# The opening of a gated-attention kernel: first four outputs from transposed strips of their own score panels, with the weights and v of batch 1 loaded later and z of batch 1 transposed later

## The chip, the cores and the metric

The kernel runs on one core of one Trainium2 chip. The metric is device time in microseconds (us) of one execution, inputs and outputs in HBM. Each comparison runs both kernels several times on the same chip. A run is called slow here when it is over 1.5% above the fastest run of the same kernel in its comparison. The granted clock is the share of TensorE's full clock that the profile shows as allowed.

Names: PE is the TensorE matmul engine, DVE is VectorE, ACT is ScalarE, POOL is GpSimd, SP is SyncE. SP issues the DMA transposes, POOL issues almost all loads and stores. In profile lines, PEld is PE's loading of weights, SPq is SP's DMA queue, and L12 is line 12 of that kernel, so one source line has different numbers in different kernels.

## The reference, cut to what matters

Batch 8, sequence S = 3136, model width 256, score width 64, rank 32.

```python
scores = (z @ z^T) / S                    # symmetric, 3136 x 3136, per batch
attn   = maximum(scores, 0) ** 2
x      = u * (attn @ v)                   # gated attention
h      = x^T @ U @ V                      # rank-32 mixing over the sequence
y      = x + h^T
out    = y + maximum(y @ w_ch1, 0) @ w_ch2
```

## The kernel before

The sequence is cut into 25 tiles of 128 rows (the last has 64). The scores are symmetric, so a panel `A[j]` holds only 13 of the 25 blocks of its row: its own and the next 12, wrapping round. For output tile o, 13 blocks come straight from stored panels, and the other 12 come from a DMA transpose of the panel of o itself, called a strip. Work goes by output tile in the order 12, 13, ..., 24, 0, ..., 11; the position in that order is called `i`. "Tile 24" below means output o = 24, which stands at position 12; a load or transpose "at tile 12" means at position i = 12. In the code NT = 25, NF = 24, HALF = FIRST = 12, P = 128 and B = 8. The mixer and the two large products of batch b run inside the attention of batch b + 1.

```python
def score(b, parts):                    # scores into PSUM, then relu on ACT, square on DVE
    ps = pair_psum()
    ...                                 # cut: one or two matmuls from zT
    for dst, src in todo:
        nc.scalar.activation(out=dst, in_=src, func=AF.Relu, scale=sc)
    for dst, _ in todo:
        nc.vector.tensor_tensor(out=dst, in0=dst, in1=dst, op=ALU.mult)

def turn(b, o):                         # a strip: 12 blocks transposed by DMA, on SP's queue
    strip = strip_pool.tile([P, HALF, P], BF16, name="strip")
    transpose(out=strip, in_=A[o][:, P:])
    strips[b, o] = strip

def block(b, o, j):
    k = (o - j) % NT
    return A[j][:, k * P : (k + 1) * P] if k <= HALF else strips[b, o][:, NT - 1 - k, :]
```

The opening of batch 0 (`start_up`) makes outputs 12 to 15 from freshly scored columns, without strips, and puts a marker on SP's queue that holds the first strips until batch 1's first v parts have landed. The large loads are issued near its top.

```python
def start_up():
    parts = ((8, 16), (0, 8), (16, NF))
    first_z(parts[:2])
    ...                                 # cut: identity, v of batch 0, z turned on PE
    if B > 1:
        load_z(1, WHOLE)
    run(fetches)                        # w1, U, V, two halves of w2: 1.4 MB in the SBUF types
    if B > 1:
        for part in V_PARTS[:3]:
            load_v(1, part)             # 3 x 192 KB
    ...
    pairs = [(8, 9), (10, 11), (12, 13), (14, 15), (6, 7), (3, 4), (5,), (1, 2)]
    pairs += [(0, 16), (17, 18), (19, 20), (21, 22), (23, 24)]
    ...
    for i, pair in enumerate(pairs):
        if i == 5 and B > 1:            # the marker
            nc.sync.dma_start(out=mark, in_=v_both[1][:1, V_PARTS[2][1] - 1, :8])
        ...
        make(pair)
        if i > 5 and i % 2:
            nxt.pop(0)()
        if i > 1:
            use(pairs[i - 2], outs)
    ...                                 # cut: outputs 16 to 19, from panels and strips
        if B > 1 and i in (1, 2):       # z of batch 1, doubled and transposed here, issued at 40 to 44 us
            part = ((0, FIRST), (FIRST, NF))[i - 1]
            double_z(1, (part,))
            turn_z(1, (part,))
```

After the opening each batch runs its tiles with one strip issued per tile, four tiles ahead. From tile 13 the panels of the next batch are scored among the attention matmuls, which needs the transposed z (`zT`) of that batch:

```python
for i in range(begin, NT):              # begin = 8 in batch 0
    o = turns(i)
    fill = [s for key in own.get(i, ()) for s in score_steps(b, *key)]
    if more:
        fill += [s for key in next_at[i] for s in score_steps(b + 1, *key)]   # from i = 13
        if b and i == 7:
            turn_z(b + 1, ((FIRST, NF),))
        if b and i == 10:
            turn_z(b + 1, ((0, FIRST),))
        ...
    _spread(attend_steps(b, o), fill)
    if i + AHEAD < NT:
        turn(b, turns(i + AHEAD))
```

Of the kernel before, what the change touches and what calls it, by code (L numbers as in the profile page):

```python
# [42 lines left out]
def kernel(  # L43
# [156 lines left out]
    def first_z(parts):  # L200

        z_bf = z_tiles[0] = stage.tile([P, NT, 2, dqk], BF16, name="z_bf")
        wide = zT_rest[:, :4, :].rearrange("p t c -> p (t c)")
        nc.vector.memset(wide, 0.0)
        ps = pair_psum()
        for _ in range(7):
            mm(out=ps[:, 0, :], lhsT=zT_rest[:, 0, :], rhs=wide, start=True, stop=True)
        landed = []
        for t0, t1 in parts:
            z_f = u_pool.tile([P, 2, D], FP32, name="u_sb").rearrange("p a c -> p (a c)")  # L210
            z_f = z_f.rearrange("p (t c) -> p t c", c=dqk)
            nc.sync.dma_start(out=z_f, in_=rows(z[0])[:, t0:t1, :])
            landed.append(z_f)
        for (t0, t1), z_f in zip(parts, landed):
            nc.vector.tensor_copy(out=z_bf[:, t0:t1, 0, :], in_=z_f)
            nc.scalar.copy(out=z_bf[:, t0:t1, 1, :], in_=z_f)

    def turn_on_pe(parts, banks):

        z_bf = z_tiles[0]  # L220
        for (t0, t1), ps in zip(parts, banks):
            for t in range(t0, t1):
                mm(
                    out=ps[:, (t - t0) * P : (t - t0 + 1) * P],
                    lhsT=z_bf[:, t, :, :].rearrange("p h c -> p (h c)"),
                    rhs=eye,
                    start=True,
                    stop=True,
                )
            copy = nc.vector.tensor_copy if t0 % 8 or t1 == NF else nc.scalar.copy  # L230
            copy(
                out=zT_first[:, t0:t1, :].rearrange("p t c -> p (t c)"),
                in_=ps[:, : (t1 - t0) * P],
            )
# [424 lines left out]

    def start_up():  # L660
        parts = ((8, 16), (0, 8), (16, NF))
        first_z(parts[:2])
# [10 lines left out]
        load_v(0, (8, 12))  # L673
        load_v(0, (12, 18))
        load_z(0, parts[2:])
        for part in [(3, 8), (0, 3), (18, NF), (NF, NT)]:
            load_v(0, part)
        turn_on_pe([(8, 12), (12, 16)], sets[0])
        turn_on_pe([(0, 4), (4, 8)], sets[1])
        nc.gpsimd.memset(U_bf[:, NF, :], 0.0)  # L680
        outs = [FIRST + i for i in range(NG)]
        c0 = FIRST * P
        for o in outs[::2]:
            open_pair(0, o)
            load_u(0, o)
        if B > 1:
            load_z(1, WHOLE)
        run(fetches)
        if B > 1:
            for part in V_PARTS[:3]:  # L690
                load_v(1, part)
        nxt = [s for j in range(LEAD, LEAD + NG) for s in turned(0, j)]
        rooms = [A[j % NT][:, : 2 * NG * P] for j in range(LEAD + NG, LEAD + 3 * NG)]
        rooms = [r.rearrange("p (a w) -> p a w", a=2) for r in rooms]
        pairs = [(8, 9), (10, 11), (12, 13), (14, 15), (6, 7), (3, 4), (5,), (1, 2)]
        pairs += [(0, 16), (17, 18), (19, 20), (21, 22), (23, 24)]
        where = {}
        mark = small.tile([P, D], BF16, name="mark", tag="t1_sb")[:1, :8]

        def make(pair):  # L700
            if all(LEAD - 1 - HALF <= j < FIRST for j in pair):
                todo = []
                for j in pair:
                    at = (FIRST - j) * P
                    where[j] = A[j][:, at : at + NG * P]
                    todo.append((j, c0, NG * P, where[j]))
                score(0, todo)
            else:
                room = rooms.pop(0)
                for i, j in enumerate(pair):  # L710
                    where[j] = room[:, i, :]
                score(0, [(j, c0, NG * P, room) for j in pair])

        def use(pair, some):
            for j in pair:
                for o in some:
                    at = (o - FIRST) * P
                    stop = [o % 2 == 1 and j == NF - h for h in range(2)]
                    beside(o, j, where[j][:, at : at + P], stop)

        for i, pair in enumerate(pairs):
            if i == 5 and B > 1:

                nc.sync.dma_start(out=mark, in_=v_both[1][:1, V_PARTS[2][1] - 1, :8])
            if i == 3:
                double_z(0, parts[2:])
            if i == 5:
                turn_on_pe([(16, NF)], [pair_psum().rearrange("p a w -> p (a w)")])
                turn_on_pe([(NF, NT)], [pair_psum()[:, 0, :]])
                extend_z(0)  # L730
            make(pair)
            if i > 5 and i % 2:
                nxt.pop(0)()
            if i > 1:
                use(pairs[i - 2], outs)

        for o in outs[1::2]:
            nxt.pop(0)()
            for pair in pairs[-2:]:
                use(pair, (o - 1, o))  # L740
            close_pair(0, o)

        outs = [LEAD + i for i in range(NG)]
        for o in outs[::2]:
            open_pair(0, o)
            load_u(0, o)
        pairs = [(j, j - 1) for j in range(LEAD - 1, LEAD - FIRST, -2)]

        def use_stored(js, some):
            for j in js:  # L750
                for o in some:
                    if 0 <= o - j <= HALF:
                        beside(o, j, block(0, o, j))

        def make_stored(pair):
            todo = []
            for j in pair:
                k0, k1 = LEAD - j, min(NB, LEAD + NG - j)
                todo.append((j, LEAD * P, (k1 - k0) * P, A[j][:, k0 * P : k1 * P]))
            score(0, todo)  # L760

        nxt += [lambda pair=pair: make_stored(pair) for pair in pairs[:2]]
        run(nxt[:2])
        own = [
            lambda j=j, some=some: use_stored([j], some)
            for some in (outs[:2], outs[2:])
            for j in outs
            if j <= some[-1]
        ]
        run(_merge(nxt[2:], own))  # L770
        rest = []
        for j in reversed(range(FIRST - NG, LEAD)):
            rest += score_steps(0, j, LEAD + NG - j, NB)
        more = [s for j in range(LEAD + NG, LEAD + 2 * NG - 1) for s in score_steps(0, j)]
        for i, pair in enumerate(pairs):
            if i + 2 < len(pairs):
                make_stored(pairs[i + 2])
            else:
                more.pop(0)()
            use_stored(pair, outs)  # L780
            if B > 1 and i in (1, 2):
                part = ((0, FIRST), (FIRST, NF))[i - 1]
                double_z(1, (part,))
                turn_z(1, (part,))
            if i == len(pairs) - 1:
                turn(0, LEAD + NG)
        tail = []
        for o in outs:
            js = [(o + 1 + i) % NT for i in range(HALF)]

            def close(o=o, j=js[-1]):
                beside(o, j, block(0, o, j), [o % 2 == 1] * 2)
                if o % 2:
                    close_pair(0, o)
                if o == outs[1]:
                    load_u(0, LEAD + NG)
                if o < outs[-2]:
                    turn(0, o + NG + 1)

            for i in range(3):  # L800
                some = js[4 * i : min(4 * i + 4, HALF - 1)]
                tail.append(lambda o=o, js=some: [beside(o, j, block(0, o, j)) for j in js])
            tail.append(close)
        for s in _merge(tail, more + rest):
            s()
# [9 lines left out]
    first_at = {8: [(NT - 2, 0, NB), (0, 0, NB)], 9: [(NT - 1, 0, NB)], 10: [(1, 0, NB)]}  # L815
    first_at.update({11: [(2, 0, NB)], 12: []})
    for j, i in zip(range(3, FIRST), (10, 11, 11, 12, 12, 12, 12, 12, 12)):
        first_at[i].append((j, 0, FIRST - j))
    first_turns = {8: (NT - 2,), 9: (NT - 1, 0)}
# [13 lines left out]
    puts = dict(zip((13, 14, 15, 16, 17, 18), puts))  # L833
    late = []
    for b in range(B):
# [5 lines left out]
        v_at = dict(zip((9, 11, 13, 15, 18, 21), V_PARTS[3:]))  # L841
        ahead = dict(zip((2, 3, 6, 7, 10, 11, 14), range(NC)))
        for i in range(begin, NT):
            o = turns(i)
            fill = [s for key in own.get(i, ()) for s in score_steps(b, *key)]
            if more:
# [3 lines left out]
                if b and i == 7:  # L850
                    turn_z(b + 1, ((FIRST, NF),))
                if b and i == 10:
# [3 lines left out]
                if i == 11:  # L856
                    extend_z(b + 1)
            main = attend_steps(b, o)
# [3 lines left out]
            if b == 0 and i in first_turns:  # L862
                for t in first_turns[i]:
                    turn(b, t)
            elif i + AHEAD < NT:
# [74 lines left out]
```

## Time and profile before

| | before |
|---|---|
| time, median of 3 runs | 1004.49 us (1002.80 to 1008.39) |
| span of the profiled run | 1003.0 us, granted clock 1.00 |
| first matmul of tile 24 of batch 0 | 62.7 us |
| first rank matmul of batch 0 (attention of batch 0 is over) | 106.8 us |
| first matmul of tile 24 of batch 1 | 166.3 us |

The last rows are milestones: the start of the first matmul of one source line in one batch, read from the trace. The same work stands between two of them in either kernel.

First, the profile page's line of busy time by engine, kernel before:

```profile
PE 984.2 (98%) x13688; PEld 776.2 (77%) x13688; DVE 550.6 (55%) x1002; ACT 612.3 (61%) x835; POOL 171.8 (17%) x317
```

PE is busy all but 19 us. That number bounds what can be won by closing gaps.

Next, the windows view of the kernel before: a stretch in us, its length, then busy us (and instructions) of PE, its weight loads, DVE, ACT and POOL, the granted clock, the DMA share, and GB/s moved. The DMA share is the time that packets took, over the time of 16 engines; packets overlap, so it can pass 1.

```profile
core 0: us, PE busy (x) PEld busy (x) DVE busy (x) ACT busy (x) POOL busy (x), PEclk, DMA share, GB/s
5.00:20.00 15.00, 11.46 (x162) 8.91 (x162) 10.57 (x21) 11.81 (x19) 7.87 (x15) 1.00 1.04 188
20.00:35.00 15.00, 13.05 (x191) 9.83 (x188) 12.99 (x28) 14.49 (x24) 3.45 (x6) 1.00 1.00 177
35.00:60.00 25.00, 20.75 (x328) 16.28 (x326) 17.73 (x36) 18.68 (x28) 3.25 (x6) 1.00 1.27 197
60.00:85.00 25.00, 24.45 (x428) 19.54 (x426) 18.77 (x39) 19.05 (x30) 4.36 (x7) 1.00 1.21 209
85.00:110.00 25.00, 25.00 (x451) 21.13 (x449) 17.98 (x32) 17.45 (x24) 5.65 (x9) 1.00 1.17 187
250.00:350.00 100.00, 99.84 (x1435) 80.40 (x1432) 52.60 (x97) 59.94 (x82) 19.08 (x36) 1.00 0.92 174
```

More than half of PE's idle time lies before 60 us: 15.00 - 11.46 = 3.5 us, then 2.0, then 4.3 (another 5.4 us lie after 900).

The waits of PE in the first 70 us (us in total, times, longest), and one wait of SP's DMA queue:

```profile
PE ps L298 <- ACT A L311: 3.3, 5, 1.0
PE ps L371 <- DMA strip<-A: 2.7, 2, 2.1
PE ps L371 <- DVE A L313: 2.0, 4, 0.9
PE ps L371 <- DMA v<-in_v_dram: 0.8, 1, 0.8
```

```profile
SPq L724 <- DMA v<-in_v_dram: 29.4, 1, 29.4
```

L298 is the score matmul, L371 attention, L724 the marker. The last line shows that the marker keeps SP's queue closed for 29.4 us.

### The profile page before, as it was taken

The page shows a single profiled execution, that of the slowest core. Times are in us where ns is not written, and L with a number is a line of the kernel's source. Part 1 is how long each engine was busy: PE and PEld are TensorE (multiplying, and loading weights), DVE is VectorE, ACT ScalarE, POOL GpSimd, SP SyncE. Part 2 cuts the span into 40 slices and gives each one's busy share as a digit, 9 for nine tenths or more (in the row PEclk, how much of TensorE's full clock was granted, in tenths as well). Part 3 has the DMA queues.
Part 4 walks back from the last instruction along what each step waited for, and adds up shares of the span by engine and source line. Part 5 has one row for each costly group of instructions (what it writes and reads, how often), then busy time and mean ns, then how long its engine had stood idle before and what let it go on. Part 6 is the DMA issues. An engine that isn't in the chain of part 4 may idle for free.

```text
span 1003.0 us, 31017 instructions
## 1 busy us (share of the span) xinstructions
PE 984.2 (98%) x13688; PEld 776.2 (77%) x13688; DVE 550.6 (55%) x1002; ACT 612.3 (61%) x835; POOL 171.8 (17%) x317
## 2 busy tenths in 40 slices
PE   7899999999999999999999999999999999999998
PEld 5678777787778877788787887778878788777855
DVE  6868754457544665456644566445663457542342
ACT  7877764667645776466755667466664667633154
POOL 5111112111121211221112211112111120011000
PEclk9999999999999999999999999999999999999999
DMA  9999989999798999999999997989989998678442
GB/s 177 186 196 206 175 153 186 169 198 173 149 205 165 170 160 181 178 179 168 156 185 174 188 162 149 192 177 179 170 156 181 181 183 152 127 152 166 99 98 97
DMA packets 414646, 167.94 MB, mean 167 GB/s; under 512 B 389472, under 2 KB 399136, under 8 KB 414512
## 3 DMA queue, kind: packets, MB, share of 16 engines
q1 hardware_dynamic: 385280, 99.68, 62.9%
q0 software_dynamic: 29232, 66.28, 28.5%
q8 instruction: 107, 1.75, 0.7%
q14 instruction: 27, 0.22, 0.1%
HBM read 61.88 MB, written 25.69 MB: 87 GB/s over the span
## 4 chain that ended last, share of the span: by engine, by line
PE 90%; DVE 4%; ACT 3%; DMA 2%; issue 0%; POOL 0%; DVEq 0%; ACTq 0%; POOLq 0%
PE ps L371 46%; PE ps L608 17%; PE ps L563 17%; PE ps L298 6%; ACT A L311 3%; DVE A L313 1%; PE ps L405 1%; DMA strip<-A 1%; DVE x_bf L545 1%; PE ps L531 1%; DMA z_c<-in_z_dram 1%; PE ps L479 1%; DMA zT<-z_bf 1%; DVE both L386 1%; DVE x_bf L395 0%
## 5 line engine op out<-in xcount | busy, mean ns | idle before, releaser
L311 ACT ACTIVATE A<-ps 128x832 bf16<-128x832 f32 (+9 forms) x477 | 359.1, 768 | 156.1 <-PE ps L298 149.6
L371 PE MATMUL ps<-v,A 64*128 64x256 bf16 x4988 | 341.8, 270 | 2.4 <-DVE A L313 1.1
L313 DVE TENSOR_TENSOR A<-A 128x832 bf16<-128x832 bf16 (+9 forms) x477 | 244.6, 527 | 131.2 <-ACT A L311 128.0
L371 PE MATMUL ps<-v,strip 64*128 64x256 bf16 x4420 | 307.4, 269 | 3.6 <-DMA strip<-A 2.7
L371 PEld LDWEIGHTS <-A 64*128 64x128 bf16 x4988 | 246.8, 94 | 45.8 <-issue 11.2
L581 ACT ACTIVATE relu_bf<-ps 128x1024 bf16<-128x1024 f32 (+2 forms) x206 | 186.0, 911 | 140.8 <-PE ps L563 138.7
L371 PEld LDWEIGHTS <-strip 64*128 64x128 bf16 x4420 | 222.8, 94 | 37.4 <-DMA strip<-A 4.6
L619 DVE TENSOR_TENSOR o_sb<-ps,x_bf 128x512 f32<-128x512 f32 (+1 forms) x104 | 69.7, 670 | 246.2 <-PE ps L608 223.8
L608 PE MATMUL ps<-w_bf,relu_bf 128*128 128x256 bf16 (+1 forms) x1600 | 201.5, 273 | 0.2 <-ACT relu_bf L579 0.2
L563 PE MATMUL ps<-ut,w_bf 128*128 128x512 bf16 (+2 forms) x896 | 198.3, 353 | 1.1 <-DVE x_bf L545 1.0
L608 PEld LDWEIGHTS <-relu_bf 128*128 128x128 bf16 (+1 forms) x1600 | 152.3, 98 | 46.6 <-issue 4.6
L563 PEld LDWEIGHTS <-w_bf 128*128 128x128 bf16 x896 | 85.0, 98 | 63.4 <-issue 7.7
L355 POOL DMA_DIRECT2D u_sb<-in_u_dram x96 | 53.7, 559 | 456.1 <-DVE x_bf L395 440.8
L298 PE MATMUL ps<-zT 64*128 64x416 bf16 (+8 forms) x812 | 131.7, 312 | 0.0
L385 ACT COPY both<-ps 128x512 f32<-128x512 f32 (+1 forms) x104 | 58.9, 566 | 73.8 <-PE ps L371 66.4
L632 POOL DMA_DIRECT2D out_dram<-o_sb x84 | 46.0, 548 | 278.2 <-DVE o_sb L619 274.9
L386 DVE TENSOR_TENSOR both<-ps,both 128x512 f32<-128x512 f32 (+1 forms) x104 | 69.4, 667 | 27.5 <-ACT both L385 26.7
L395 DVE TENSOR_TENSOR x_bf<-both,u_sb 128x512 bf16<-128x512 f32 (+1 forms) x104 | 69.8, 672 | 3.6
L545 DVE TENSOR_TENSOR x_bf<-ps,x_bf 128x512 bf16<-128x512 f32 (+1 forms) x112 | 65.4, 626 | 8.1 <-PE ps L531 8.0
L298 PEld LDWEIGHTS <-zT 64*128 64x128 bf16 x812 | 43.2, 94 | 3.9
L244 POOL DMA_DIRECT2D v<-in_v_dram x61 | 34.1, 561 | 1.2 <-DMA w_bf<-in_moe_w_ch_dram 1.1
L298 PE MATMUL ps<-relu_bf 64*128 64x416 bf16 (+9 forms) x121 | 22.2, 332 | 4.1 <-ACT A L311 3.3
(54 smaller groups left out, 207.9 us busy)
## 6 DMA issues: line engine op xcount, KB each, us to landing
u_sb<-in_u_dram POOLq DMA_DIRECT2D x96, 256.0 KB, 4.1
out_dram<-o_sb POOLq DMA_DIRECT2D x84, 256.0 KB, 3.2
v<-in_v_dram POOLq DMA_DIRECT2D x57, 192.0 KB, 5.1
strip<-A SPq DMA_TRANSPOSE x196, 5.6
out_dram<-o_sb SPq DMA_DIRECT2D x12, 256.0 KB, 2.0
z_c<-in_z_dram POOLq DMA_DIRECT2D x7, 384.0 KB, 5.7
u_sb<-in_u_dram POOLq DMA_DIRECT2D x16, 64.0 KB, 2.9
ut<-x_bf SPq DMA_TRANSPOSE x56, 3.6
```

The costliest lines, as they stand in the source:

```text
L298: mm(out=ps[:, k, :n], lhsT=zT[halves[k], j, :], rhs=zT_flat[halves[k], c : c + n], start=True, stop=True,)
L311: nc.scalar.activation(out=dst, in_=src, func=AF.Relu, scale=sc)
L313: nc.vector.tensor_tensor(out=dst, in0=dst, in1=dst, op=ALU.mult)
L371: mm(out=acc[t0][h][:, (o - t0) * D : (o - t0 + 1) * D], lhsT=w[halves[h]], rhs=v_both[b % 2][halves[h], j, :], start=start, stop=stop, **kw,)
L385: nc.scalar.copy(out=both[:, :w], in_=banks[1][:, :w])
L386: nc.vector.tensor_tensor(out=both[:, :w], in0=banks[0][:, :w], in1=both[:, :w], op=ALU.add)
L395: nc.vector.tensor_tensor(out=x_at(b, t0, n), in0=split(both[:, :w]), in1=u_sb[:, :n, :].rearrange("p t (a c) -> p t a c", c=P), op=ALU.mult,)
L545: nc.vector.tensor_tensor(out=q, in0=split(ps[h][:, : len(ks) * D]), in1=q, op=ALU.add)
L563: mm(out=ps[i][:, :w] if apart else ps[:, i, :w], lhsT=w1_bf[:, db, (hp + i) * P : (hp + i + 1) * P], rhs=uT[c][:, db, len(chunks[c]) * P ...
L581: nc.scalar.activation(out=relus[c][:, hp : hp + 2, :w], in_=ps[:, :, :w], func=AF.Relu)
L608: mm(out=ps[r, k * D : (k + 1) * D], lhsT=relus[c][:, ht, q : q + (TAIL if two else P)], rhs=w2_bf[:, ht, :], start=(ht < 1 + two), stop=( ...
L619: nc.vector.tensor_tensor(out=o_sb[:p, :nk, :].rearrange("p t (a c) -> p t a c", c=P), in0=split(ps[:p, : nk * D]), in1=x_at(b, t, nk)[:p] ...
```

## The change

The intent is to drop the columns that the old opening scores only for outputs 12 to 15, and to build these outputs from panels 12 to 15, which have to be made anyway, and their strips. To give these early strips quick passage, loads leave the opening: the weights, three parts of v and the z transposes of batch 1. The marker goes. The diff, cut to its core:

```diff
     def start_up():
-        parts = ((8, 16), (0, 8), (16, NF))
-        first_z(parts[:2])
+        casts = first_z(((8, 16), (16, NF), (0, 8), (NF, NT)))   # z of batch 0 all on SP's queue
...
-        run(fetches)
-        if B > 1:
-            for part in V_PARTS[:3]:
-                load_v(1, part)
+        run(casts[:2])
+        turn_on_pe([(8, 12), (12, 16)], sets[0], (act, vec))
+        turn_on_pe([(16, 20), (20, NF)], sets[1], (act, vec))
+        casts[3]()                                               # the last 64 rows of z
...
-        pairs = [(8, 9), (10, 11), (12, 13), (14, 15), (6, 7), (3, 4), (5,), (1, 2)]
-        pairs += [(0, 16), (17, 18), (19, 20), (21, 22), (23, 24)]
-                nc.sync.dma_start(out=mark, in_=v_both[1][:1, V_PARTS[2][1] - 1, :8])
+        make((8, 9), FIRST)
+        turn_on_pe([(NF, NT)], [sets[1][0]], (vec,))
+        casts[2]()
+        make((10, 11), FIRST)
+        steps = [panel[12][0], use((8, 9)), turn_rest, panel[12][1], use((10, 11))]
+        ...                                                      # panels 13 to 17, strips 12 to 15
...
-            if B > 1 and i in (1, 2):
-                part = ((0, FIRST), (FIRST, NF))[i - 1]
-                double_z(1, (part,))
-                turn_z(1, (part,))
...
-    puts = dict(zip((13, 14, 15, 16, 17, 18), puts))
+    later = {(0, 12): fetches[1], (0, 13): fetches[2], (0, 23): fetches[0]}   # U, V, w1
+    later.update({(1, 2): fetches[3], (1, 3): fetches[4]})                    # w2
+    puts = dict(zip((17, 18, 19, 20, 21, 22), puts))
...
-        v_at = dict(zip((9, 11, 13, 15, 18, 21), V_PARTS[3:]))
+        v_at = dict(zip((10, 11, 12, 14, 15, 17, 18, 20, 21), V_PARTS))
...
-                if b and i == 7:
+                if b == 0 and i == 9:
+                    double_z(b + 1, ((FIRST, NF), (0, FIRST)))
+                if i == (7 if b else 10):
                     turn_z(b + 1, ((FIRST, NF),))
-                if b and i == 10:
+                if i == (10 if b else 11):
                     turn_z(b + 1, ((0, FIRST),))
+            if (b, i) in later:
+                later[b, i]()
```

## The prediction

> **What bounds the kernel now.** TensorE: the page gives PE 984.2 us busy of a 1003.0 us span, clock 1.00. By the windows view the first 60 us have 10.99 us without PE work, 60 to 70 us 0.55, the last 103 us 5.35, the rest almost none. The Trainium skill ("Perfetto Trace Analysis", Identifying the Most-Contended Engine) warns that PE busy time doesn't show nearness to roofline; I use only its gaps. An opening change can win these 11 us plus work removed.
>
> The waits view names them: scores waiting for ScalarE to empty PSUM 3.3 us, attention waiting for a transposed strip 2.7 (2.08 of it at 50 us, when two z transposes of batch 1 stood before strip 20), for VectorE's squares 2.0, first matmul 1.3, v 0.8, z_bf and relu_bf copies 1.2. SyncE held its first strip until 31.9 us, behind a marker DMA that waited 29.4 us for batch-1 v.
>
> **What the change does.**
> - Replaces five column score pairs for outputs 12 to 15 (j = 16 to 24 and 0) by the own panels 12 to 15, which have to be made anyway. By instruction order: 9 fewer score matmuls, 6,912 fewer streamed columns; at 0.22 us for two 512-column row halves, about 1.5 us of PE. ScalarE loses about 6,500 columns, at 0.88 us per 1024 about 5.6 us.
> - Adds four strip transposes (5.6 us median to landing, some 2.6 us apart when queued) and two DVE casts (0.43 us each).
> - Moves weights and three parts of batch-1 v (about 2 MB) out of the first 30 us, the batch-1 z transposes to tiles 10 and 11, and drops the marker.
>
> **How much is critical.** I walked the new order by hand with traced durations (ScalarE 0.53/0.76/0.88 us for 512/832/1024 columns; PE 0.109 us per block of two half matmuls). From 6 to 20 us ScalarE limits: panels 12 to 15 cost it 6.1 us and give PE only ten blocks at once. I expect 5 to 7 us of PE idle there, no better than before (3 to 4). Strip 12 should be issued near 11.5 us and land near 17.5, strip 15 near 25; outputs 12 to 15 end near 27 us, as before, but with panels 12 to 17 complete. The second four then run nearly dense: start-up ends near 43 us instead of 46. The 2.08 us wait at 50 us goes, perhaps the 0.9 us wait at 58 too. The rank matmuls of batch 0 (first at 106.8 us before) should start near 101.5. From there nothing changes; w2, loaded two tiles before use, should be in time.
>
> **Predicted: 998.5 us, 8 in 10 between 994 and 1003.** Faster by over 2%: 0.01 (20 us isn't there to win). Within: 0.97. Slower: 0.02.
>
> **What would show it.** PE idle in 5 to 20 us about 5 to 7 us, waiting for ScalarE and VectorE; idle in 27 to 60 us below 2 us (before, about 5); no strip wait over 1 us after 30 us; rank matmuls 4 to 6 us earlier; the time after them unchanged within 1 us.
>
> **What would make it wrong.** All DMAs run on the same 16 engines and interleave ("DMA: Bandwidth & Descriptors", Issuing engines are not separate DMA queues). If strips 12 to 15 share them with late v and batch-1 z and land in 9 us rather than 5.6, PE waits 3 to 5 us more and the gain is gone. If late weights or z are not there in tiles 10 to 12 or in batch 1, a new wait appears after 70 us.

## The result, and the profile after

The changed kernel took 1042.11 us in the median of four runs (1030.30 to 1048.84), the kernel before 1003.81. The ratio is 1.0295, with a 95% interval of 1.0238 to 1.0353: slower by about 3%. Ratios here and below come from the fast runs of both kernels, so they are not quite the ratios of the medians quoted. Two of the four runs of the changed kernel were left out as slow; with them the ratio of the means is 1.036, as in r1 below, where none was left out.

The lag of the changed kernel at each milestone, from the two traces (spans 1036.0 and 1003.0 us):

| milestone | before | after | lag | added since the row above |
|---|---|---|---|---|
| tile 24, batch 0 | 62.7 | 63.8 | 1.1 | 1.1 |
| rank, batch 0 | 106.8 | 125.3 | 18.5 | 17.4 |
| tile 24, batch 1 | 166.3 | 189.4 | 23.1 | 4.6 |
| rank, batch 1 | 228.0 | 251.0 | 23.0 | -0.1 |
| tile 24, batch 2 | 287.6 | 316.0 | 28.4 | 5.4 |
| rank, batch 2 | 349.3 | 380.3 | 31.0 | 2.6 |
| tile 24, batch 3 | 408.9 | 441.2 | 32.3 | 1.3 |
| end | 1003.0 | 1036.0 | 33.1 | 0.8 |

The rewritten opening cost one microsecond in this trace, no more than traces of one opening differ by: before, r9, r10 and r18, which are alike up to position 10, have tile 24 at 61.4 to 63.0. From tile 24 to rank, before and r10 agree (44.1). More than half of the loss came in 44 us of batch 0 whose arithmetic had not been touched.

The busy time and the windows after, to be read against those of before:

```profile
PE 990.2 (96%) x13639; PEld 780.0 (75%) x13679; DVE 547.2 (53%) x1000; ACT 606.5 (59%) x829; POOL 169.4 (16%) x314
```

```profile
5.00:20.00 15.00, 8.99 (x85) 5.66 (x84) 7.79 (x17) 6.76 (x12) 3.18 (x7) 0.77 0.94 185
20.00:35.00 15.00, 13.12 (x200) 9.72 (x198) 10.27 (x20) 11.80 (x21) 0.54 (x1) 1.00 0.71 129
35.00:60.00 25.00, 22.77 (x370) 18.46 (x367) 18.73 (x41) 19.80 (x32) 2.37 (x5) 1.00 1.03 180
60.00:85.00 25.00, 9.94 (x159) 6.45 (x157) 6.38 (x13) 7.66 (x14) 4.10 (x8) 0.74 1.20 136
85.00:110.00 25.00, 25.00 (x406) 20.37 (x404) 17.51 (x36) 17.64 (x26) 6.45 (x11) 0.92 1.14 189
250.00:350.00 100.00, 94.16 (x1236) 73.61 (x1237) 50.13 (x94) 56.69 (x76) 16.33 (x30) 0.97 0.96 158
```

ACT's busy time fell by 5.8 us, as predicted, but PE's waits for ACT fell only from 3.3 to 2.2 us. In 20 to 35 us the DMA share is 0.71 where it was 1.00: the opening now leaves DMA time unused. In 60 to 85 us PE worked 9.94 of 25 us, with the DMA share at 1.20 and only 136 GB/s moved. So the engines' time was taken, and little came of it.

The waits of PE over the whole run name the stops:

```profile
PE ps L308 <- DMA zT<-z_bf: 14.5, 1, 14.5
PE ps L234 <- DVE z_bf L224: 5.4, 1, 5.4
PE ps L415 <- DVE x_bf L555: 5.4, 4, 3.8
PE ps L381 <- DVE o_sb L629: 2.9, 2, 1.5
PE ps L573 <- DMA ut<-x_bf: 2.8, 1, 2.8
```

L308 is the score matmul, L234 the turning of z on PE, L415 tile 24, L573 the first large product. Three of these bear on the early loss: one wait of 14.5 us for the second half of batch 1's transposed z, one of 5.4 us in the opening, one of 2.8 us for the first transposed x (`ut`) of batch 0. The strip waits of the opening are gone. The other two lines (tile 24's wait for `x_bf`, attention's for `o_sb`) stand at 300 us and later.

The longest wait, seen on SP's queue (start, length of issue), then POOL's, then on PE, where the bracket gives the idle time before and its releaser:

```profile
66.03 5.61 SPq L195 DMA_TRANSPOSE zT<-z_bf  x1
```

```profile
60.83 1.13 POOL L254 DMA_DIRECT2D v<-in_v_dram  x2
61.93 0.56 POOL L267 DMA_DIRECT2D U_bf<-in_moe_U_dram  x1
66.92 0.58 POOL L365 DMA_DIRECT2D u_sb<-in_u_dram  x1 [3.90 <-DVE x_bf L405]
67.49 0.52 POOL L271 DMA_DIRECT2D relu_bf<-in_moe_V_dram  x1
```

```profile
83.43 0.23 PE L308 MATMUL ps<-zT 64*128 64x64 bf16 x2 [14.50 <-DMA zT<-z_bf]
```

The transpose was issued at 66.03 us, among v, U, u and V loads, and PE went on at 83.43. Its time from issue to landing, and that of the two such transposes of the kernel before (issued at 40 to 44 us):

```profile
DMA to landing us min/median/max: 8.0/12.7/17.3
```

```profile
DMA to landing us min/median/max: 4.3/5.1/5.9
```

And the same ten microseconds of both traces, first after, then before:

```profile
73.00:83.00 10.00, 0.00 (x0) 0.00 (x0) 0.00 (x0) 0.00 (x0) 0.00 (x0) 0.50 1.14 71
```

```profile
73.00:83.00 10.00, 10.00 (x180) 8.55 (x176) 8.92 (x18) 7.04 (x11) 1.52 (x3) 1.00 1.17 214
```

Every compute engine stands still and the DMA share is no smaller than before, but 71 GB/s are moved instead of 214. From the queue tables of these ten microseconds (1,239 packets of SP's queue after and 5,552 before, for 71.4% and 77.7% of the engines' time) a packet of about 250 bytes took some 92 ns instead of 22. The V load, issued 1.5 us after the transpose, was as slow: 15.7 us to landing, where it took 7.1 in the opening of before. The clock reads 0.50 there and stays so until about 89 us, five and a half microseconds after work resumed. At half speed that costs about 2.7 us more, so 14.5 + 2.7 = 17.2 of the 17.4 us are explained. The Trainium skill ("TensorE: Matmul & The Clock Gate", Part 1) says that an idle window of about 3.4 us halves the clock, and that about 3.4 us of sustained work restore it, counted in windows that run on whatever the kernel does; the trace agrees on the fall (PE stopped at 68.9, the clock was 0.52 in 72 to 74 us), while the return took longer.

The wait in the opening, on DVE and on PE:

```profile
11.84 0.20 DVE L222 CAST z_bf<-both 128x64 bf16<-128x64 f32 x1 [4.90 <-DMA both<-in_z_dram]
12.19 0.29 PE L234 MATMUL ps<-eye,z_bf 128*128 128x128 bf16 x1 [5.44 <-DVE z_bf L224]
```

The last 64 rows of z, 16 KB, are loaded last on SP's queue (twice, once for each half of the partitions), and they landed some 9 us after their issue at 2.8 us, beside the v loads. PE waited 5.44 us, and again its clock read 0.50, until about 17.5 us. Strip 12, which I had expected to be issued at 11.5 us, was issued at 18.1.

### The profile page after: what moved, and what is told of

It reads as the page before. It is cut to its first block, busy times and chain, and to the rows that moved or that the text cites. A ratio compares the mean times of both kernels' runs of the same rounds, so it can differ in the third digit from the quotient of the medians.

```text
span 1036.0 us, 30957 instructions
## 1 busy us (share of the span) xinstructions
PE 990.2 (96%) x13639; PEld 780.0 (75%) x13679; DVE 547.2 (53%) x1000; ACT 606.5 (59%) x829; POOL 169.4 (16%) x314
## 3 DMA queue, kind: packets, MB, share of 16 engines
q1 hardware_dynamic: 391840, 101.55, 61.7%
## 4 chain that ended last, share of the span: by engine, by line
PE 86%; DMA 6%; DVE 4%; ACT 2%; issue 1%; SPq 0%; POOL 0%; DVEq 0%; ACTq 0%; POOLq 0%
PE ps L381 44%; PE ps L618 16%; PE ps L573 16%; PE ps L308 6%; DMA zT<-z_bf 4%; ACT A L321 2%; DVE x_bf L555 1%; DVE A L323 1%; PE ps L415 1%; PE ps L541 1%; DMA both<-in_z_dram 1%; DMA out_dram<-o_sb 1%; DMA ut<-x_bf 1%; DVE both L396 1%; DVE x_bf L405 1%
## 5 line engine op out<-in xcount | busy, mean ns | idle before, releaser
L321 ACT ACTIVATE A<-ps 128x832 bf16<-128x832 f32 (+9 forms) x472 | 353.1, 761 | 164.9 <-PE ps L308 159.2
L381 PE MATMUL ps<-v,strip 64*128 64x256 bf16 x4512 | 314.0, 270 | 0.0
L323 DVE TENSOR_TENSOR A<-A 128x832 bf16<-128x832 bf16 (+9 forms) x472 | 240.7, 523 | 133.8 <-ACT A L321 130.8
L381 PEld LDWEIGHTS <-A 64*128 64x128 bf16 x4896 | 242.1, 95 | 52.6 <-issue 13.5
L381 PEld LDWEIGHTS <-strip 64*128 64x128 bf16 x4512 | 228.5, 94 | 34.0
L573 PE MATMUL ps<-ut,w_bf 128*128 128x512 bf16 (+2 forms) x856 | 197.9, 354 | 6.0 <-DMA ut<-x_bf 2.8
L308 PE MATMUL ps<-zT 64*128 64x416 bf16 (+8 forms) x812 | 131.9, 313 | 14.5 <-DMA zT<-z_bf 14.5
L573 PEld LDWEIGHTS <-w_bf 128*128 128x128 bf16 x896 | 85.6, 98 | 67.3 <-issue 9.3
L395 ACT COPY both<-ps 128x512 f32<-128x512 f32 (+1 forms) x104 | 58.8, 565 | 82.8 <-PE ps L381 68.9
L308 PEld LDWEIGHTS <-zT 64*128 64x128 bf16 x812 | 43.2, 94 | 18.9 <-DMA zT<-z_bf 14.8
L541 PE MATMUL ps<-t_sb,V_bf 64*128 64x256 bf16 x200 | 22.9, 270 | 1.1 <-DVE x_bf L555 1.1
```

What stands on the lines that cost most here:

```text
L308: mm(out=ps[:, k, :n], lhsT=zT[halves[k], j, :], rhs=zT_flat[halves[k], c : c + n], start=True, stop=True,)
L381: mm(out=acc[t0][h][:, (o - t0) * D : (o - t0 + 1) * D], lhsT=w[halves[h]], rhs=v_both[b % 2][halves[h], j, :], start=start, stop=stop, **kw,)
L395: nc.scalar.copy(out=both[:, :w], in_=banks[1][:, :w])
L573: mm(out=ps[i][:, :w] if apart else ps[:, i, :w], lhsT=w1_bf[:, db, (hp + i) * P : (hp + i + 1) * P], rhs=uT[c][:, db, len(chunks[c]) * P ...
```

## The experiments

The theory after reading the traces (A): the change moved DMA work out of an opening that could bear it into the tail of batch 0 and the start of batch 1, where the kernel before already drives the DMA engines hardest; the transposes that PE needs there then land late. Three rivals: the place (the loss is the place of the z transposes alone, one tile less slack), any load (any extra load there costs as much), and the opening (the new opening itself is slow).

The expectations use letters. A, and E in other words, are the theory above. B: a transfer stalls at random. C: the loads of U and V slowed the z transpose. D: the place. F: the late z and v of batch 1 do it. G: the kind of load decides, not the amount. H: strips and loads beside each other slow both. I: bunched loads are what hurts.

All runs in one table. "24" and "rank" are the milestones of batch 0 in the profiled run, in us (before: 62.7 and 106.8, 44.1 apart).

| run | kernel | ratio to before | 95% interval | 24 | rank |
|---|---|---|---|---|---|
| r1_repeat | after, unchanged | 1.0358 | 1.0303 to 1.0412 | 62.5 | 141.1 |
| r2_tail_first | after, last z rows first | 1.0266 | 1.0191 to 1.0340 | 63.8 | 135.0 |
| r8_tail_later | after, last z rows used later | 1.0221 | 1.0174 to 1.0267 | 61.6 | 125.4 |
| r4_z_early | after, z transposes two tiles earlier | 1.0257 | 1.0199 to 1.0315 | 65.0 | 119.0 |
| r3_uv_late | after, U and V later | 1.0278 | 1.0203 to 1.0353 | 63.4 | 131.0 |
| r5_w_open | after, weights in the opening | 1.0215 | 1.0165 to 1.0265 | 69.6 | 120.0 |
| r7_uv_open | after, U and V in the opening | 1.0151 | 1.0090 to 1.0212 | 62.4 | 112.7 |
| r6_before_w_late | before, weights late | 1.0098 | 1.0045 to 1.0151 | 59.2 | 112.7 |
| r11_before_z_late | before, z transposes as in after | 1.0050 | 1.0016 to 1.0085 | 60.1 | 111.1 |
| r13_before_z_at_8 | before, z transposes at tiles 8, 9 | 1.0020 | 0.9992 to 1.0048 | 62.9 | 107.0 |
| r12_before_no_mark | before, without marker | 1.0076 | 1.0045 to 1.0108 | 68.1 | 114.2 |
| r9_extra_b0 | before, 448 KB of useless loads, spread | 1.0013 | 0.9981 to 1.0045 | 61.7 | 107.4 |
| r10_extra_b3 | the same in batch 3 | 1.0004 | 0.9978 to 1.0030 | 61.4 | 105.5 |
| r18_extra_bunched | before, 384 KB of useless loads in two | 1.0049 | 1.0009 to 1.0088 | 63.0 | 115.2 |
| r14_strips_old_loads | new opening, old load schedule | 1.0183 | 1.0152 to 1.0214 | 79.2 | 124.5 |
| r17_after_pieces_only | after, weights in 12 pieces | 1.0272 | 1.0203 to 1.0340 | 62.8 | 123.5 |
| r15_after_pieces | pieces, z early, last z rows later | 1.0065 | 1.0039 to 1.0092 | 61.3 | 107.8 |
| r16_before_pieces | before, weights in 12 pieces, late | 1.0035 | 0.9991 to 1.0079 | 62.5 | 106.5 |

The profiled runs of r3 and r8 were of the slow kind by the rule above; single milestones of profiled runs vary by a few us between runs of these kernels.

Many sizes foretold were missed. r2 won nothing in the opening. r3 had C's short landing but not its 12 to 18 us. r5 ended above its 1004 to 1018 us, r6 between E's 15 to 35 us and F's 5, r12 on H's side, r14 on H's side with more loss than foretold, r15 between its two theories. r9 is a miss for theory E itself, and r16, which was to be faster, was not.

### r1_repeat: the changed kernel once more

No edit.

> The changed kernel once more, nothing edited: do the same waits come back? Theory A (the new order itself causes them): the 5.4 us wait for the z tail near 12 us, the wait of over 10 us for the z transpose near 83 us, and the wait for the first transposed x group near 142 us all come back within 2 us. Rival B (a transfer stalls at random): the sum over 1003 us stays 25 to 45 us but the waits stand at other places.

Median 1040.42 us (1037.25 to 1048.11). The three waits came back: 16.4 us for zT, 4.9 for the last z rows, 2.7 for `ut`. But 11.0 us of waits for ACT (which itself waited 17.2 us for strip transposes) joined them between 60 and 160 us, and batch 0's stretch from tile 24 to the rank matmuls took 78.6 us. After tile 24 of batch 1 it lost nothing more (lag 43.2 there, 43.4 at the end), so the late losses of the first trace, at 300 us and on, are not a fixed part of the change. The early ones are.

### r2_tail_first and r8_tail_later: the wait in the opening

r2 issues the last rows of z first on SP's queue; r8 leaves the load where it is and casts and turns the rows later in the order.

```diff
 # r2
-        for n, (t0, t1) in enumerate(parts):
+        for n, (t0, t1) in sorted(enumerate(parts), key=lambda e: e[1][0] != NF):
...
-        return casts
+        return casts[1:] + casts[:1]
 # r8
-        casts[3]()
...
-        turn_on_pe([(NF, NT)], [sets[1][0]], (vec,))
-        casts[2]()
...
+        def turn_tail():
+            casts[3]()
+            turn_on_pe([(NF, NT)], [pair_psum()[:, 0, :]], (vec,))
+
+        steps = [panel[12][0], use((8, 9)), casts[2], turn_rest, use((10, 11)), turn_tail, panel[12][1]]
```

> The z tail (64 rows) is the first z transfer on the SyncE queue instead of the last. Theory A: it lands before 5 us, the 5.4 us wait near 12 us and the slow clock of 10 to 17 us go, first scores may start 1 us later; 5 to 8 us faster than the changed kernel, the wait near 83 us stays. Rival (the tail is slow because it is made of 64-row pieces, wherever it stands): it still lands after 9 us and nothing is won.

> The changed kernel with the z tail's cast and turn placed later in the instruction order (just before the second half of panel 12), the transfers unchanged. Theory: the first scores, panel 12's first half and the blocks of j = 8 to 11 fill the time in which the tail is on its way; the 5 us wait near 12 us falls to under 2.5 us, PE keeps its clock, first quarter matmul at 58 to 61 us instead of 62.5 to 65. The rest of the kernel, and its waits after 63 us, as changed: 1025 to 1045 us.

r2 won nothing in the opening: its first z cast ran at 6.86 us (before: 3.6), PE waited 5.4 us for the larger z parts instead, and tile 24 came at 63.8 as in after. The parts of z issued after the last rows landed 4.8 us and more after their issue, beside the v loads. r8 took the wait down to two of 0.8 us in all, and tile 24 came at 61.6. That is the new opening without its mishap: about 1 us better than the trace of before, not 5, and within the 61.4 to 63.0 of the old opening's traces. And the time did not follow (1.0221): in the profiled run, a slow one, batch 0 waited 16.8 us for zT and 10.3 for strips as if nothing had happened.

### r4_z_early and r3_uv_late: moving one culprit in batch 0

```diff
 # r4
-                if b == 0 and i == 9:
+                if b == 0 and i == 8:
                     double_z(b + 1, ((FIRST, NF), (0, FIRST)))
-                if i == (7 if b else 10):
+                if i == (7 if b else 8):
...
-                if i == (10 if b else 11):
+                if i == (10 if b else 9):
 # r3
-    later = {(0, 12): fetches[1], (0, 13): fetches[2], (0, 23): fetches[0]}
+    later = {(0, 16): fetches[1], (0, 17): fetches[2], (0, 23): fetches[0]}
...
-    puts = dict(zip((17, 18, 19, 20, 21, 22), puts))
+    puts = dict(zip((19, 20, 21, 22, 23, 24), puts))
```

> Only the batch-1 z transposes move, from tiles 10 and 11 to 8 and 9 (their copies from tile 9 to 8); U and V stay at 12 and 13. Theory C: the transposes have landed before these loads start, the wait near 83 us goes, 12 to 18 us are won; something else queued then (a strip, or the u load) may still be slow but has four tiles of slack. Rival D also expects the wait to go, so this run alone does not part them; it tells whether the loads of U and V hurt anything else: if the end is still over 1025 us, they do.

> Only the loads of U and V move, from tiles 12 and 13 to 16 and 17 (and V's copies from 17..22 to 19..24). Theory C (the z transpose took 17 us because these two loads shared the DMA engines with it): the z transpose lands in under 8 us, the wait for it falls from 14.5 to under 4 us, and 12 to 18 us are won. Rival D (too little slack: the transpose stands one tile before its use whatever else is loaded): the wait stays over 8 us, under 6 us are won.

PE's waits between 60 and 160 us, first r4, then r3:

```profile
PE ps L381 <- DMA strip<-A: 11.2, 3, 7.1
PE ps L573 <- DMA ut<-x_bf: 3.6, 1, 3.6
PE ps L308 <- ACT A L321: 3.3, 3, 2.6
```

```profile
PE ps L308 <- ACT A L321: 15.8, 3, 9.3
PE ps L381 <- DMA strip<-A: 5.0, 1, 5.0
PE ps L308 <- DMA zT<-z_bf: 3.6, 1, 3.6
```

In r4 the zT wait is gone, in r3 it fell from 14.5 to 3.6 us (landing in 6.8 us). Neither won back the time: other transposes were late in their place. But r3 shows what made the z transpose slow. Eight traces of the changed kernel and its variants have z at tiles 10 and 11. Where whole U and V loads stand at tiles 12 and 13, the slower half of z took 14.4 to 19.8 us to land (after, r1, r2, r8). Where U and V come later (r3), in the opening (r5, r7) or in halves at other tiles (r17), it took 6.9 to 7.5. PE still waits 3.3 to 4.5 us for zT in these last four. In r3 PE's wait reads "ACT", but ACT itself was waiting: 17.7 us in two waits for strip transposes, as it may not overwrite a panel that a transpose is still reading. The rival of the place alone falls with r4. In r3 PE's waits for ACT end at 103 and 113 us, after the U and V loads at their new place (issued at 82 to 84 us). That fits theory A but doesn't show it: r1, whose loads had not moved, has waits of the same kind.

### r5_w_open and r7_uv_open: loads back into the opening

```diff
 # r5: run(fetches); r7: run(fetches[1:3])
             load_z(1, WHOLE)
+        run(fetches)
...
-    later = {(0, 12): fetches[1], (0, 13): fetches[2], (0, 23): fetches[0]}
-    later.update({(1, 2): fetches[3], (1, 3): fetches[4]})
+    later = {}                                   # r7 keeps w1 and w2 here
```

> The changed kernel with all five weight loads back in the opening, right after the batch-1 z load; everything else as changed. Theory E (loads on the GpSimd queue that run beside strip transposes slow these, and the strips, z and x transposes are what PE then waits for; the weights are 1.4 MB of such loads): the waits for z near 83 us, for strips and x groups near 140 to 160 us and for ScalarE near 110 to 133 us all go; from the first quarter matmul (o = 24) to the first rank matmul 44 to 48 us as before the change instead of 54 to 79; but the opening is slower by 3 to 10 us, as strips 12 to 15 now run beside the weights. End 1004 to 1018 us. Rival F (the late batch-1 z and v loads do it): the waits after 63 us stay and the end is over 1025 us.

> The changed kernel with only U and V back in the opening; w1 at tile 23, w2 at tiles 2 and 3 of batch 1. Theory E: the wait near 83 us falls under 4 us (12 to 20 us won), the waits between 110 and 165 us stay (5 to 15 us); end 1008 to 1022 us. If U and V are harmless the wait near 83 us stays.

Both gave a wrong output, by my mistake: U's last rows are loaded before the instruction that zeroes that tile. r14 puts that instruction first and is right. The times stand, as the work is the same. With U and V back (r7), zT waited 3.6 us, and batch 0 took 50.3 us from tile 24 to rank instead of 61.5; the ratio fell to 1.0151. With all weights back (r5) that stretch took 50.4 us, but the opening took 69.6, with strip waits of 1.9 and 3.8 us: the loads and the new early strips do not get on. The opening that needs strips early and the loads want the same stretch of DMA time.

### r6, r11, r13, r12: one part of the change on the kernel before

```diff
 # r6_before_w_late: the weights alone, at the places of after
-        run(fetches)
...
+    later = {(0, 12): fetches[1], (0, 13): fetches[2], (0, 23): fetches[0]}
+    later.update({(1, 2): fetches[3], (1, 3): fetches[4]})
+    puts = dict(zip((17, 18, 19, 20, 21, 22), puts))
 # r11_before_z_late: the z transposes alone, at tiles 10 and 11 as in after
-            if B > 1 and i in (1, 2):
-                part = ((0, FIRST), (FIRST, NF))[i - 1]
-                double_z(1, (part,))
-                turn_z(1, (part,))
...
+                if b == 0 and i == 9:
+                    double_z(b + 1, ((FIRST, NF), (0, FIRST)))
+                if i == (7 if b else 10):
 # r13_before_z_at_8: the same, doubled at tile 8, transposed at 8 and 9
 # r12_before_no_mark: the marker alone
-                nc.sync.dma_start(out=mark, in_=v_both[1][:1, V_PARTS[2][1] - 1, :8])
```

> The kernel before, with this one part of the change alone: weights at tiles 12, 13, 23 of batch 0 and 2, 3 of batch 1 (V's copies at 17 to 22). Theory E: 15 to 35 us slower than before, with new waits after 63 us that trace back to transposes. Rival F: within 5 us of before, or faster by the up to 3 us that the earlier marker gives.

> The kernel before with this one part alone: batch-1 z doubled at tile 9 and transposed at tiles 10 and 11, extended at 12; weights and the marker as before. If the late z by itself is harmful (its second half is used two tiles later in batch 0, three in others): a wait for z near 68 to 75 us of 3 to 6 us, 3 to 8 us slower. If it hurt only together with the late weights: no z wait over 1 us, and up to 2 us faster, as strip 20 no longer waits 2.08 us.

> The kernel before with batch-1 z doubled and transposed at tiles 8 and 9 instead of in the opening (or at 10 and 11, as in r11). If the late z cost 5 us only for want of slack: no z wait over 1 us, and the opening keeps the 1 to 2 us that r11 won there; 0 to 3 us faster than before. If any later z costs: 3 us slower or more.

> The kernel before without the marker DMA alone, so that strips 16 to 19 are transposed while the weights and batch-1 v still load. Theory E: little, -2 to +4 us (strips start earlier but share the engines with the loads). Theory H (mixing ruins both): over 5 us slower, strips 16 to 19 landing after 8 us or more.

r6 is the clearest. Its opening became 3.5 us shorter (59.2), and then batch 0 gave back 9.4 us: 53.5 instead of 44.1 from tile 24 to rank. The wait of PE, and what ACT was doing:

```profile
PE ps L298 <- ACT A L311: 7.1, 1, 7.1
PE ps L563 <- DMA ut<-x_bf: 3.7, 2, 2.1
```

```profile
75.45 2.00 ACT L311 ACTIVATE A<-ps 128x384 bf16<-128x384 f32 x3 [9.06 <-DMA strip<-A]
```

So late weights alone, with no new opening, no moved z and no moved v, make strips late in batch 0 (landing in up to 15.1 us between 60 and 80 us), and PE stops for them. The new opening falls as the sole cause.

r11 gives one wait of 5.3 us for zT, whose two halves landed in 7.1 and 8.2 us. With the weights loaded in the opening the transpose takes 8.2 us at most and not 17.3, and it is still too late: tile 11 for a use in tile 13 has too little slack. Two tiles earlier (r13, landed in 5.8 us) there is no such wait and no measurable loss. So the place of z is worth 0.5%, and the rest of the 14.5 us in after (9.2) is about what the landing was slower (17.3 - 8.2 = 9.1).

r12 shows what the marker is for. Without it the strips start beside the loads and land in a median of 7.3 us and up to 18.6 (before, in the same 20 to 60 us: 5.9 and 8.0); between 20 and 60 us PE waits:

```profile
PE ps L371 <- DMA strip<-A: 6.9, 3, 6.0
```

### r9, r10, r18: useless loads

```diff
 # r9_extra_b0 (r10_extra_b3: b == 3); four loads of 112 KB, never read
+            if b == 0 and i in (11, 12, 13, 14):
+                pool_dma(out=spill, in_=moe_w_ch1[:P, :448])
 # r18_extra_bunched: two loads of 192 KB
+            if b == 0 and i in (12, 13):
+                c = NZ + (i - 12) * H
+                pool_dma(out=idle[R:, c : c + H], in_=moe_w_ch1[(i - 12) * 96 : (i - 11) * 96, :])
```

> The kernel before, with four useless loads of 112 KB (448 KB in all, about what U and V are) at tiles 11 to 14 of batch 0, into a tile that nothing reads. Theory E (batch 0 after the opening is a stretch in which the DMA engines are full: share 1.17 to 1.27 there against 0.80 to 1.07 in a later batch, so every load added there is paid by PE): 2 to 8 us slower than before, quarter to rank matmuls of batch 0 46 to 52 us instead of 44.1. Rival G (it is the kind of load, V's 32 long rows and the weights' short ones, not the amount): no change beyond 1.5 us.

> The same four useless loads at tiles 11 to 14 of batch 3. Theory E: DMA has room there, under 1.5 us slower than before. If any load beside transposes costs PE time wherever it stands (theory H, mixing), it costs as much as in batch 0.

> The kernel before with two useless loads of 192 KB at tiles 12 and 13 of batch 0, where the change puts U and V (and as many bytes), in long rows of w1, into a place that nothing reads; r9 spread as much over four tiles at no clear cost. Theory I (bunching): 2 to 8 us slower, quarter to rank matmuls 46 to 52 us. If only V's and U's own kind of load hurts, or the tight order of the changed kernel is needed too: under 2 us.

Spread over four tiles, 448 KB cost batch 0 1.6 us in the profile and nothing that the times can tell from zero. In batch 3 the same loads cost nothing either. In two larger loads at tiles 12 and 13, 384 KB cost 0.5%, with 52.2 us from tile 24 to rank, and PE waits between 63 and 160 us of

```profile
PE ps L298 <- ACT A L311: 5.5, 3, 3.1
```

The rival of any load falls with r9. So does the plain form of my own theory, which foretold 2 to 8 us for r9: a high DMA share alone doesn't make every added load costly. That bunching is what matters is suggested by r18, but the intervals of r9 (0.9981 to 1.0045) and r18 (1.0009 to 1.0088) overlap, so it isn't shown.

### r14_strips_old_loads: the new opening beside the old loads

The new opening with weights and v of batch 1 where they were, z at tiles 8 and 9 and the last z rows used later, so that neither known wait disturbs.

```diff
+        nc.gpsimd.memset(U_bf[:, NF, :], 0.0)
+        run(fetches)
+        if B > 1:
+            for part in V_PARTS[:3]:
+                load_v(1, part)
...
+    later = {}
+    puts = dict(zip((13, 14, 15, 16, 17, 18), puts))
...
+        v_at = dict(zip((9, 11, 13, 15, 18, 21), V_PARTS[3:]))
```

> The new opening (outputs 12 to 15 from strips of their own panels) with the loads where they were before the change: weights and three parts of batch-1 v right after batch-0 v, the other parts at tiles 9 to 21, V's copies at 13 to 18; z at tiles 8 and 9 and the tail turned later. Theory H (strips beside a run of loads are slow): strips 12 to 15 wait 4 to 10 us in the opening, first quarter matmul at 66 to 73 us; after it nothing unusual, 44 to 46 us to the rank matmuls; end 1007 to 1016. If the new opening is good by itself: first quarter matmul before 61 us and the end under 1002 us.

The ratio is 1.0183. Most of it lies in the opening (tile 24 at 79.2, 16.5 of the 19.0 us at the end); from there to rank it took 45.3 us, 1.2 more than before. The granted clock was 0.70 in 20 to 35 us and 0.84 in 35 to 60. Two waits for strips:

```profile
32.25 2.74 PE L381 MATMUL ps<-v,strip 64*128 64x256 bf16 x23 [6.48 <-DMA strip<-A]
41.41 1.89 PE L381 MATMUL ps<-v,strip 64*128 64x256 bf16 x16 [5.43 <-DMA strip<-A]
```

The landing times of strips issued between 10 and 45 us, first in after (nine strips), where the opening's loads are gone, then in r14 (four), where they are back:

```profile
DMA to landing us min/median/max: 3.7/4.0/5.9
```

```profile
DMA to landing us min/median/max: 4.4/14.0/20.7
```

A transpose of the same size lands in 4.0 us in the median with the opening's loads gone and in 14.0 us beside them. The loads suffer as well. Issued in the same 10 to 45 us, the v loads took 18.6 us in the median in r14 and 7.6 in before, where the marker keeps the strips away from them; V took 14.2 us instead of 7.1. The Trainium skill ("DMA: Bandwidth & Descriptors", Queues, rings and completion order) says that each DMA engine goes round its queues packet by packet. The page's queue table of the kernel before has 385,280 packets for 99.68 MB on SP's queue, 259 bytes each, and 29,232 for 66.28 MB on POOL's, 2.3 KB each. If small packets take turns with large ones, a transpose of many small ones waits long; that this is how the 14.0 us arise is not shown, and it doesn't say why the large loads were slower too. The skill says that transposes are as fast as regular DMAs ("Advanced Engine Details and Errata", X-Bar Transpose). The traces agree in so far as strips and loads fare alike: 4.0 us for a strip of 384 KB and 4.2 for a u load of 256 KB in after; in r14 both are slow, 14.0 us for strips and 14.2 to 18.6 for the loads of V, w2 and v.

### r17, r15, r16: the loads in small pieces

The weights are cut into 12 loads of 96 to 128 KB, in after at tiles 8, 9, 13, 16, 19, 22, 23 and 24 of batch 0 and 0 to 3 of batch 1. r17 does this alone; r15 adds z at tiles 8 and 9 and the later use of the last z rows; r16 does the pieces on the kernel before, all in batch 0 but one.

```diff
-        fetches = [
-            lambda: wide(w1_bf, moe_w_ch1),
-            ...
+        fetches = [lambda f=f, k=k: f(k) for f, n in ((v_part, 2), (u_part, 2), (w1_part, 4), (w2_part, 4)) for k in range(n)]
...
+    later = dict(zip(((0, 8), (0, 9), (0, 13), (0, 16), (0, 19), (0, 22), (0, 23), (0, 24), (1, 0), (1, 1), (1, 2), (1, 3)), fetches))
```

> The changed kernel with only the weights in pieces; z still at tiles 10 and 11, tail still early. Theory I (bunched weight loads are the larger part): the z wait near 83 us falls from 14 to 16 us to 3 to 6 us, as in r7 and r11, waits after 90 us under 4 us; 1012 to 1022 us. If most of r15's gain was the earlier z and the later tail: over 1025 us.

> The changed kernel with the weights in twelve pieces of 96 to 128 KB, one to a tile (batch 0: 8, 9, 13, 16, 19, 22, 23, 24; batch 1: 0 to 3), z at tiles 8 and 9, tail turned later. Theory I (what hurt was the bunching: u, v, U, V at neighbouring tiles before a transpose that is needed soon): waits after 63 us under 5 us in sum, 998 to 1008 us. Theory G (the weights' kind of load hurts in any dose): over 1015 us.

> The kernel before with the weights in the same twelve pieces, one to a tile (batch 0: 8, 10, 12, 14, 16, 17, 19, 20, 22, 23, 24; batch 1: 0). Theory I: the opening keeps the 3 us that r6 won there (quarter matmul near 59 us), the later waits of r6 (7.05 us near 76, 3.7 us near 130) fall under 3 us in sum; 1 to 4 us faster than before. Theory G: 5 to 12 us slower than before, like r6.

r15 recovers most: median 1011.55 us, ratio 1.0065; batch 0 takes 46.5 us from tile 24 to rank, and PE's waits from 60 to 160 us are small:

```profile
PE ps L319 <- ACT A L332: 2.1, 4, 0.7
PE ps L584 <- DMA ut<-x_bf: 1.9, 2, 1.0
```

It is still not faster than the kernel before. Its opening is 1.4 us shorter than in the trace of before (61.3), the two stretches after it lose 2.4 and 2.2, and the lag at the end is 6.1 us.

r17 missed its expectation. The zT wait fell to 4.5 us as expected, but strips among the w1 and w2 pieces, u and z of batch 2 landed in up to 23.5 us, and PE waited:

```profile
PE ps L392 <- DMA strip<-A: 10.6, 4, 7.4
PE ps L319 <- DMA zT<-z_bf: 4.5, 1, 4.5
```

So small pieces alone are not the cure; why r15, with the same pieces, escapes these waits is open. r16 wins nothing (1.0035) and spreads wider, from 1002.61 to 1024.03 us. No version that I ran beat the kernel before.

## Why the prediction was wrong

The step that failed is "From there nothing changes; w2, loaded two tiles before use, should be in time", with its test "the time after them unchanged within 1 us". After the opening 32.0 of the 33.1 us were lost. w2 itself was in time: no wait for it shows. I had named the risk ("If late weights or z are not there in tiles 10 to 12 or in batch 1, a new wait appears after 70 us") and priced it at nothing. The term that should have stood there: z's transpose 17.3 us from issue to landing instead of the 4.3 to 5.9 of the trace that I had, which made a 14.5 us wait and 2.7 us of half clock; then 4.6 us by tile 24 of batch 1, 2.8 of them the wait for `ut`. The last 10.0 us, from there on, are the part that r1 didn't repeat. I asked whether a moved load would be in time for its own user, and not what it would do to the transposes beside it. The windows view of the kernel before had a warning, though not a rule (r9): a DMA share of 1.17 to 1.27 from 35 to 110 us.

Point by point:

- "An opening change can win these 11 us plus work removed." True as an upper bound, and the source of too narrow a range: idle time limits the gain, nothing limits the loss.
- ACT 5.6 us less, fewer score matmuls: right for ACT (612.3 to 606.5 us busy), but worth little: PE's waits for ACT fell by 1.1 us.
- "5 to 7 us of PE idle" in 5 to 20 us: 6.0 measured, for another reason. It was one wait of 5.4 us for the last 64 rows of z, which I had not costed at all, and not ACT, whose waits came to 2.2 us in the whole run.
- "Strip 12 should be issued near 11.5 us and land near 17.5": issued at 18.1. The landings were better than I feared (4.0 us in the median, not 5.6), as the loads had left.
- "The second four then run nearly dense", "the 2.08 us wait at 50 us goes": right. PE idle in 35 to 60 us fell from 4.3 to 2.2 us, and in 27 to 60 us, where below 2 was foretold, from 5.6 to 2.4.
- "Start-up ends near 43 us instead of 46", hence rank 4 to 6 us earlier: wrong. Tile 24 came 1.1 us later than before. With the last z rows out of the way (r8, r15) it came 1.1 to 1.4 us earlier, so even the mechanism that I believed in was worth at most about a quarter of what I gave it, and traces of the old opening differ by as much. The old opening with the weights taken out came at 59.2 in its one trace (r6), but at 62.5 with the weights in pieces from tile 8 on (r16).
- "If strips 12 to 15 share them with late v and batch-1 z": the worry was right (same engines, from the skill's "Issuing engines are not separate DMA queues"; r14 has 14.0 against 4.0 us), the place was wrong. It did not happen to strips 12 to 15 but to what came after them.

What was shown, from the parts taken singly on the kernel before: weights late +1.0%, z transposes late +0.5%, no marker +0.8%; the new opening beside the old loads +1.8%; the whole change about +3%. Shown, too, is that the loads of U and V made the z transpose of the changed kernel slow (14.4 to 19.8 us to land with them beside it, 6.9 to 7.5 without). The change trades one shortage for another: its strips need the DMA engines early, so loads have to leave, and where they go transposes stand that PE soon needs.

What stays open: why the DMA engines moved only 71 GB/s from 73 to 83 us; whether size, number or kind of the loads decides (r9 against r18; no run added a load of V's kind, 32 long rows, by itself); what the later v of batch 1 costs, which no run moved alone; why the pieces work in r15 and not in r17; and the changed kernel's irregular losses from batch 2 on (8 us in batch 2 and 10 by the end in one trace, none in the repeat).

## What to carry to other kernels

When a change moves loads, look at the transfers that run in the stretch they move into, above all those that PE soon waits for; a load that is in time for its own user can still make a neighbour late. This kernel, with PE busy 98% of its span, had at most 19 us of idle time to win and lost over 30, so the range needed a long upper side. A wait that reads as another engine's may be a DMA's: follow it one step further, as with ACT waiting to overwrite a panel whose strip is not yet read.

## What the Trainium skill lacked or had wrong

- "Advanced Engine Details and Errata" (X-Bar Transpose) calls transposes as fast as regular DMAs and doesn't say that the two together can both be slow. Here the strips landed in 4.0 us in the median with the opening's loads gone and in 14.0 us beside them (up to 20.7), while the loads of V, w2 and v took 14.2 to 18.6 us instead of 7.1 to 7.8 in the kernel before; the slower half of z took 17.3 us beside the loads of U and V instead of 6.9 to 7.5 without them.
- "DMA: Bandwidth & Descriptors" (Issuing engines are not separate DMA queues) says that transfers interleave, but gives no price for it. In 73 to 83 us the DMA share was 1.14 in one kernel and 1.17 in the other, for 71 and 214 GB/s; the section doesn't tell how to know such a stretch beforehand.
- The same page doesn't mention that a small load on SP's queue suffers too: 16 KB of z took about 9 us beside the v loads.
- "TensorE: Matmul & The Clock Gate" (Part 1) gives about 3.4 us of sustained work for the clock to return. After both long waits (5.4 and 14.5 us) the granted clock stayed at 0.50 for more than 5 us of work (12.2 to about 17.5 us, and 83.4 to about 89).
